# Two attention blocks on one core: two tiles of exponentials in eight computed as a cubic on VectorE and GpSimd, and weights loaded in pieces

## The chip, the cores and the metric

One core of one Trainium2 chip. The time is the device time of one execution in microseconds (us). Engines are named as in the profile: PE (TensorE matmuls), PEld (its weight loads), ACT (ScalarE), DVE (VectorE), POOL (GpSimd), SP (the queue that issues most DMAs).

## What is computed

Two independent blocks over 2048 positions, 1024 features and 32 heads of 32 channels; their outputs are put side by side.

```python
# A: plain attention
q, k, v = split(x @ wqkv)                       # 32 heads
p = softmax(q @ k.T * 32 ** -0.5)               # 2048 x 2048 for each head
out_a = (p @ v) @ wo

# B: four segments of 512 positions, causal inside a segment, with a memory M, z carried over segments
phi = lambda t: where(t > 0, t + 1, exp(t))
a_dot = softmax(q_s @ k_s.T * scale + mask) @ v_s
a_mem = (phi(q_s) @ M) / (phi(q_s) @ z + 1e-6)
o = g * a_mem + (1 - g) * a_dot                 # g = sigmoid(beta)
M = M + phi(k_s).T @ v_s;  z = z + sum(phi(k_s))
out_b = o @ wo
```

The inputs are normal numbers times 0.05 in bf16; the weights of B have another factor of 1/32. Scores are therefore small: for A half the scale times (largest |q|^2 + largest |k|^2) of a group of four heads is between 0.077 and 0.090, worked out from the reference's inputs.

## The kernel before

**Tiles and sets.** Heads are taken four at a time: a group g of A (8 groups) or an index j of B (8 in each of 4 segments). A *unit* of A is a group and a chunk c of 256 queries (64 units); it runs over eight key blocks t of 256 keys. One key block of one unit is a *set*: four tiles, one for each head, each of 128 x 512 scores (two pieces of 128 keys by 256 queries). `plan_set` plans a set: one PE step of eight score matmuls (L821) into four PSUM banks, then two ACTIVATEs with exp (`plan_exp`, L853), each over two banks (1024 columns for A; for B, 1024 or 768), which write bf16 to a ring of 12 buffers P, then the P·V matmuls (L898) and the row sums with a matrix of ones (L904, `plan_pv`). When a unit's last set is done, `norm` transposes the row sums on DVE (L922), takes the reciprocal (L931), spreads it (L933) and multiplies. Units of B lie between those of A. Some of B's tiles are masked on POOL (L864).

**PSUM.** Banks 0 to 5 are three slots of two banks for scores, used in turn: a set takes two slots, so the next set takes the third slot and the first slot of this set. Bank 6 is the only one for *jobs* (projections, output products, guards, memory); a job holds it from its first matmul until DVE has copied it out (L1051 for most; the matmuls have the line of the helper `mm4`, L519). Bank 7 collects P·V and the row sums of a unit.

**Order.** Nothing is ordered by the hardware at run time. The Python program gives each operation a duration, a key and its dependencies, and `schedule` plays the engines forward in a model: PE prefers a score step when it is due (ROW_LEAD ahead of ACT's end), else the best ranked P·V step or job. What comes out is a fixed queue for each engine with semaphore waits. `level` spreads the jobs between their earliest and latest times, `plan_jobs` gives these times; a DMA with `gate=True` waits for the exponential nearest to its key, and all such DMAs go through SP in order.

**Guard.** Exponentials need no maximum subtracted while scores are small. `guard_end` bounds the scores of a group by half the scale times (largest |q|^2 + largest |k|^2). Where the bound exceeds FREE = 40, a flag is raised, ACT branches to a second copy of its program with a bias in each exponential (`alt` in `plan_exp`, `run_split`), and stays there. `square` (L1069, POOL) and the first matmuls of `guard_cols` (L1078) feed it.

**Loads.** The four x_B segments are turned by a DMA transpose (L1035), Wv_B is loaded in halves of 1 MB (`load_WBv`, L1026), W_B in pieces of 256 KB (`load_WB`, L1020). Wo_B (2 MB) is loaded once and stays; Wo_A (2 MB) goes in three DMAs into tiles that are free by then (`load_WoA`). Results leave by `job_out` (L1404) and, for A's attention, through a scratch in HBM (L985).

Of the kernel before, what the change touches and what calls it, by code (L numbers as in the profile page):

```python
# [25 lines left out]
P_RING = 12  # L26
EXP_FIXED = 0.051
FREE = 40.0
# [9 lines left out]
B_STEP3 = 1.133  # L38
# [100 lines left out]
ROW_LEAD = 0.735  # L139
AHEAD = 25  # L140
HEAT = 0.605
STICK = 0.5
# [4 lines left out]
JOB_SLOPE = 0.8  # L147
MARGIN = 0.535
RXJ = 4
RX0 = 80  # L150
LEAD_A, LEAD_B, DUE_AT, DUE_SLOPE = 14.053, 28.135, 19.08, 0.447
HOLD = {}
XR = 11.698
XC = 2.432
# [4 lines left out]
class Prog:  # L159
# [42 lines left out]
    def schedule(self):  # L202
# [19 lines left out]
        for o in self.ops:  # L222
            if pend[o] == 0:
# [4 lines left out]
                            rows=sum(o.urgent is not None for o in self.ops), holder=None)  # L228
# [76 lines left out]
        while left:  # L305
            best = None
            for e, c in cand.items():
                if c:
                    t = max(free[e], min(x.ready for x in c))
                    if best is None or t < best[0]:  # L310
                        best = (t, e)
            t, e = best
            c = cand[e]
            av = [x for x in c if x.ready <= t + 1e-9]
            if e == "PE":
                av = [x for x in av if not opens(x) or opening(x) <= t + 1e-9]
                o = pick(t, av, c)
                if o is None:
                    t2 = [max(free[f], min(x.ready for x in cc)) for f, cc in cand.items() if cc and f != "PE"]
                    t2 += [x.ready for x in c if x.ready > t + 1e-9]  # L320
                    t2 += [v for v in (opening(x) for x in c if opens(x)) if t + 1e-9 < v < 1e9]
                    if t2:
                        free[e] = max(t + 0.02, min(t2))
                        continue
                    o = min(av, key=lambda x: x.key)
            else:
                o = min((x for x in c if x.ready <= t + HOLD.get(e, 0.0)), key=lambda x: x.key - (XR if x.grp is not None else 0.0))
                t = max(t, o.ready)
            d = o.dur
            if e == "PE":  # L330
                ck = clock(t)
                d /= ck
                if o.mode != st["mode"]:
                    t += SWITCH
                st["mode"] = o.mode
                st["rows"] -= o.urgent is not None
                w = o.heat
                st["recent"].append((t, t + d, w * ck))
                k = int(t // WIN)
                st["acts"][k] = st["acts"].get(k, 0.0) + d * w * ck  # L340
                if opens(o):
                    g = st["holder"] = o.grp
                    for h in (0, 1):
                        mine = [x for x in g.pe if h in x.halves]
                        if not mine:
                            continue
                        for x in last[h]:
                            if x not in mine[0].deps:
                                mine[0].deps.add(x)
                                if not x.sched:  # L350
                                    pend[mine[0]] += 1
                                    x.users.append(mine[0])
                        last[h] = [x for x in g.rd if h in x.halves]
                if o.grp is not None:
                    o.grp.left -= 1
            if e == "ACT":
                st["act_end"] = t + d
                if o.prog:
                    st["opn"] += 1
                    st["prog"] = max(st["prog"], o.key)  # L360
            o.start, o.end = t, t + d
            free[e] = o.end
            o.sched = True
            queue[e].append(o)
            c.remove(o)
            left -= 1
            for u in o.users:
                pend[u] -= 1
                if pend[u] == 0:
                    u.ready = ready_of(u) + u.margin  # L370
                    cand[u.eng].append(u)
# [4 lines left out]
    def emit(self, nc, es, block_engines, final_sems):  # L376
        sems = {e: es.enter_context(nc.semaphore("s_" + e)) for e in ("PE", "ACT", "DVE", "POOL")}
        for e in ("ACT", "DVE", "POOL"):
            for n, o in enumerate(self.queue[e]):
                o.pos = n  # L380
                o.deps |= {x for x in o.order if x.eng == e and n - x.pos <= 4}
# [105 lines left out]
class _Kernel:  # L487
# [41 lines left out]

    def build(self):  # L530
# [37 lines left out]
    def alloc(self):  # L568
# [27 lines left out]
        self.WoB = sb("Wo_B", [P, 8, D])  # L596
# [3 lines left out]
        self.r_P = [Res() for _ in range(P_RING)]  # L600
# [178 lines left out]
    def plan_set(self, take, T):  # L779
# [7 lines left out]
        for k, t in enumerate(take):  # L787
            i = bufs[k // 2]
            t["P"], t["n"] = (self.Pt[i], k % 2, self.r_P[i]), n
            self.sets.setdefault(t["set"], []).append(t)  # L790
# [35 lines left out]
        self.item(T, f)  # L826
        for k in range(2):
            self.plan_exp(take[2 * k:2 * k + 2], slots[k], bufs[k], T)
            T += 2 * w / 1200.0 + EXP_FIXED
        self.st.setdefault(take[0]["unit"], T - 2 * (2 * w / 1200.0 + EXP_FIXED))  # L830
        self.en[take[0]["unit"]] = T
        self.plan_pv(take[3], T)
        return T

    def plan_exp(self, take, slot, buf, T):
        w = take[0]["w"]
        cols = 2 * w
        banks = SLOT_BANKS[slot]
        Pt, rP = self.Pt[buf], self.r_P[buf]

        def f(key):
# [3 lines left out]
            if w == 512:  # L845
                src = self.ps[:, c0:c0 + cols]
                dst = Pt.rearrange("p b n -> p (b n)")[:, 0:cols]
            else:
# [4 lines left out]
            a = self.act(guarded if early else lambda e: e.activation(dst, src, ACT.Exp, scale=SCALE), cols, key,  # L853
                         res + [self.r_bias[bc]], [rP], fixed=EXP_FIXED)
            if not early:
                a.alt, a.flag = guarded, self.flag_of[bc]
            a.prog = True
            self.exps.append(a)
            self.exp_keys.append(key)
            nd = sum(p[4] for p in take[0]["pieces"])  # L860
            if nd:
# [3 lines left out]
                                                    channel_multiplier=-1), 2 * nd * P, key + 0.1, [rP], [rP])  # L865
# [157 lines left out]
    def load_WBv(self, s, hh, key):  # L1023
        mark([self.r_WBv], "W", s, hh)
        src = self.B_wv.rearrange("(i p) n -> p i n", p=P)[:, :, 512 * hh:512 * hh + 512]
        self.dma(lambda e: e.dma_start(self.WBv[:, :, :], src), self.sm_WBv, key, [], [self.r_WBv], lat=6.0, gate=True)  # L1026

    def load_xB(self, s, key):
        xb = self.B_x[0]
        mark([self.r_xTB], "x", s)  # L1030
        self.turn(self.xTB[:, :, :], xb[L * s:L * s + L, :], self.sm_xTB, key, [], [self.r_xTB], 5.0, 2.4, True)
# [82 lines left out]
    def guard_end(self, key, cols, nper, bias_cols, bank=None):  # L1114
# [17 lines left out]
        for k, bc in enumerate(bias_cols):  # L1132
# [7 lines left out]
                [self.r_braw], [rb])  # L1140
            nf = self.nflag
# [247 lines left out]
    def job_out(self, kind, row, half, key, lhs, rl, wo, rwo, bank=None, ev="DVE"):  # L1389
# [5 lines left out]
        assert ev == "DVE"  # L1395

        def mm(h, c, r):
            for j in range(8):
                self.pe(lambda e, j=j: self.mm4(e, src[:, c], lhs(j), wo(j)[:, 512 * half:512 * half + 512][:, c],
# [6 lines left out]

    def job_outB(self, s, tt, hf, key):
        rs = [self.r_OTB[j][tt // 2] for j in range(8)]
        holds(rs, "O", s)
        self.job_out("B", 4 * s + tt, hf, key, lambda j: self.OTB[:, j, P * tt:P * tt + P], lambda j: rs[j:j + 1],  # L1410
                     lambda j: self.WoB[:, j, :], lambda j: [self.r_WoB])
# [10 lines left out]
    def load_WoA(self, key):  # L1422
        src = self.A_wo.rearrange("(j p) n -> p j n", p=P)
        for lo, n, dst, rs in ((0, 4, self.VA[0].rearrange("p a b -> p (a b)"), [r for x in self.r_VA[0] for r in x]),
                               (4, 2, self.WA[0].rearrange("p a b c -> p (a b c)"), self.r_WA[0]),
                               (6, 2, self.WA[1].rearrange("p a b c -> p (a b c)"), self.r_WA[1])):
            mark(rs, "Wo")
            self.dma(lambda e, lo=lo, n=n, dst=dst: e.dma_start(dst.rearrange("p (j n) -> p j n", n=D), src[:, lo:lo + n, :]),
                     self.sm_WoA[(lo + 1) // 3], key, [], rs, lat=5.0, gate=True)
# [74 lines left out]
    def plan_jobs(self):  # L1504
# [18 lines left out]
        for c in range(4):  # L1523
            add(p2 + 9.0, st["A", 1, 0] - 1.0, VJ, lambda key, c=c: self.job_V0(1, c, key, None, self.a0_ge))
        self.item(200.0, lambda key: self.dma(lambda e: e.dma_start(
            self.WoB[:, :, :], self.B_wo.rearrange("(j p) n -> p j n", p=P)), self.sm_WoB, key, [], [self.r_WoB], lat=12.0, gate=True))
# [16 lines left out]
        for s in range(NSEG):  # L1543
# [7 lines left out]
            self.item(rx + 0.1, lambda key, s=s: self.load_WBv(s, 0, key))  # L1551
# [12 lines left out]
            for hh in range(2):  # L1564
                r = max(en["B", s - 1, 4 * hh + 3] + 12.0, rx + 12.0) if s else rx + 12.0
                d = SB[0] - 3.0 if hh == 0 else SB[RXJ]
                if hh:
                    self.item(max(r, SB[0] - 2.9) if s else SB[0] - 2.9, lambda key, s=s: self.load_WBv(s, 1, key))
                    r = max(r, SB[0] - 2.9 + 8.0)
                for tt in range(4):  # L1570
                    add(r, d, VJ, lambda key, s=s, tt=tt, hh=hh: self.job_VB(s, tt, hh, key))
            if s:
                for k in range(8):
                    add(end + 3.0, SB[0] - 4.0, OUT, lambda key, s=s, k=k: self.job_outB(s - 1, k // 2, k % 2, key))
# [8 lines left out]
        for k in range(8):  # L1583
            add(en["B", 3, 7] + 3.0, st["A", 7, 6], OUT, lambda key, k=k: self.job_outB(3, k // 2, k % 2, key))

        t7 = st["A", 7, 0]
        self.item(t7 - 6.0, self.load_WoA)
# [20 lines left out]
        for (r, d, c, f), (t, v) in zip(jobs, self.loads):  # L1608
            self.item(t, lambda key, d=d, f=f: self.with_due(d, f, key))

# [48 lines left out]
```

## Time and profile before

| | |
|---|---|
| median of 3 runs | 1160.54 us (1156.72 to 1161.52) |
| the profiled execution | 1161.7 us, span 1160.0 us |
| granted clock of TensorE, mean | 0.995 |
| ACT, exponentials of 1024 columns (L853) | 1080, mean duration 1157 ns |
| ACT, exponentials of 768 columns (L853) | 128, mean duration 966 ns |
| DVE, copies of a job's 512 columns (L1051) | 244, median 692 ns |
| POOL, squares of 512 columns (L1069) | 124, median 1040 ns |
| HBM read, written | 39.00 MB, 11.73 MB |

Busy time is the union of an engine's instructions, so that two that overlap count once. An ACTIVATE overlaps the next, so its duration is longer than what it costs. The ends of matmuls are modelled. "A <- B" in a list of waits means that A stood still until B was done, with the total in us, the number of times and the longest. "issue" is time in which an engine waited for nothing that the profile shows.

### The profile page before, as it was taken

What the parts mean: (1) busy time and instruction counts of PE and PEld (TensorE: products, weight loads), DVE (VectorE), ACT (ScalarE), POOL (GpSimd) and SP (SyncE); (2) the same over time, 40 slices, a digit from 0 to 9 for tenths busy, and PEclk for the clock granted to TensorE, in tenths of its full rate; (3) what the DMA queues carried; (4) which work ended last, traced back from release to release, by engine and by line L of the source; (5) the groups of instructions that cost most, each with busy time, mean ns of one, the idle gap of its engine ahead of it and who ended that gap; (6) DMA issues with size and microseconds to landing.
All of it is one profiled execution on the core that took longest, in us unless ns stands there. A gap on an engine that the chain in (4) does not pass through costs nothing.

```text
span 1160.0 us, 67207 instructions
## 1 busy us (share of the span) xinstructions
PE 1066.1 (92%) x31592; PEld 725.4 (63%) x31592; DVE 602.0 (52%) x1478; ACT 1119.1 (96%) x1256; POOL 222.0 (19%) x279
## 2 busy tenths in 40 slices
PE   7998999999999988989899999899999879999997
PEld 4665666666667656656566666566676546656575
DVE  3353454554563358656733675765526565653233
ACT  3999999999999999999999999999999989999997
POOL 1101133221230222312201330331102230100000
PEclk9999999999999999999999999999999999999999
DMA  9004341135101330032130321320131630000001
GB/s 197 8 12 107 60 117 45 15 92 124 42 15 48 78 96 17 6 90 51 34 81 25 81 54 24 73 59 16 31 77 47 179 89 9 31 31 31 31 27 49
DMA packets 163255, 66.59 MB, mean 57 GB/s; under 512 B 133792, under 2 KB 160160, under 8 KB 162976
## 3 DMA queue, kind: packets, MB, share of 16 engines
q1 hardware_dynamic: 160608, 61.50, 22.0%
q8 instruction: 247, 4.05, 1.5%
q10 hardware_dynamic: 2368, 0.79, 0.3%
q14 instruction: 32, 0.26, 0.1%
HBM read 39.00 MB, written 11.73 MB: 44 GB/s over the span
## 4 chain that ended last, share of the span: by engine, by line
ACT 70%; PE 20%; issue 4%; DVE 3%; DMA 1%; SPq 1%; POOL 0%; ACTq 0%; DVEq 0%
ACT P L853 68%; PE ps L519 11%; PE ps L821 4%; PE ps L898 3%; PE ps L904 2%; ACT PKQ_B L1323 2%; SPq L1035 1%; DMA W_B<-in_B_wk_dram 1%; DMA xT_A<-in_A_x_dram 1%; ACT P L851 0%; DVE KQ_B L1051 0%; DVE T L922 0%; DVE KQ_A L1051 0%; DVE PKQ_B L1328 0%; DVE OTst L981 0%
## 5 line engine op out<-in xcount | busy, mean ns | idle before, releaser
L853 ACT ACTIVATE P<-ps 128x1024 bf16<-128x1024 f32 (+1 forms) x1208 | 1092.2, 1137 | 17.8 <-PE ps L821 14.7
L904 PE MATMUL ps<-P,onesb 128*32 128x256 bf16 (+1 forms) x4864 | 293.0, 270 | 3.8 <-issue 3.8
L898 PE MATMUL ps<-P,V_A 128*32 128x256 bf16 x4096 | 251.0, 274 | 11.2 <-ACT P L853 9.0
L821 PE MATMUL ps<-KQ_A 32*128 32x256 bf16 x4096 | 205.2, 273 | 32.0 <-ACT P L853 24.1
L821 PEld LDWEIGHTS ps<-KQ_A 32*128 32x128 bf16 x4096 | 61.2, 92 | 146.2 <-ACT P L853 123.6
L519 PE MATMUL ps<-xT_B,W_B 128*32 128x256 bf16 x4096 | 141.2, 278 | 8.6 <-DMA W_B<-in_B_wk_dram 2.5
L864 POOL TENSOR_SCALAR_AFFINE_SELECT P<-P 128x512 bf16<-128x512 bf16 x128 | 86.6, 686 | 313.9 <-ACT P L853 309.9
L519 PE MATMUL ps<-xT_A,W_A 128*32 128x256 bf16 (+1 forms) x3968 | 136.7, 277 | 7.6 <-DVE KQ_A L1051 2.5
L898 PEld LDWEIGHTS ps<-P,V_A 128*32 128x32 bf16 x4096 | 110.5, 96 | 50.3 <-ACT P L853 21.5
L904 PEld LDWEIGHTS ps<-P,onesb 128*32 128x32 bf16 x4864 | 132.2, 97 | 9.6 <-issue 4.9
L519 PEld LDWEIGHTS ps<-xT_B,W_B 128*32 128x32 bf16 x4096 | 100.9, 97 | 38.9 <-issue 27.2
L1069 POOL TENSOR_TENSOR sqB<-KQ_B 128x512 bf16<-128x512 bf16 x64 | 68.0, 1063 | 284.9 <-DVE KQ_B L1051 254.3
L519 PEld LDWEIGHTS ps<-xT_A,W_A 128*32 128x32 bf16 x3968 | 97.1, 96 | 36.1 <-issue 19.6
L1069 POOL TENSOR_TENSOR sqA<-KQ_A 128x512 bf16<-128x512 bf16 x60 | 63.4, 1057 | 224.5 <-DVE KQ_A L1051 202.2
L1051 DVE CAST KQ_B<-ps 128x512 bf16<-128x512 f32 x64 | 44.2, 691 | 115.0 <-PE ps L519 113.2
L1051 DVE CAST outsb<-ps 128x512 bf16<-128x512 f32 x56 | 38.6, 690 | 112.0 <-PE ps L519 111.9
L922 DVE STREAM_TRANSPOSE T<-ps 128x256 f32<-128x256 f32 (+1 forms) x148 | 72.1, 487 | 43.0 <-PE ps L904 22.3
L1051 DVE CAST KQ_A<-ps 128x512 bf16<-128x512 f32 x60 | 41.5, 691 | 86.9 <-PE ps L519 86.5
L933 DVE STREAM_TRANSPOSE T<-rc 128x256 f32<-128x256 f32 (+1 forms) x152 | 73.0, 482 | 3.1
L519 PE MATMUL ps<-Wo_B,OT_B 128*32 128x256 bf16 x2048 | 73.2, 274 | 0.7 <-DVE outsb L1051 0.5
L519 PE MATMUL ps<-Wv_B,xT_B 128*32 128x256 bf16 x2048 | 69.4, 274 | 1.3 <-DVE KQ_B L1051 1.1
L519 PEld LDWEIGHTS ps<-Wo_B,OT_B 128*32 128x32 bf16 x2048 | 48.8, 96 | 18.2 <-issue 11.0
(96 smaller groups left out, 947.6 us busy)
## 6 DMA issues: line engine op xcount, KB each, us to landing
Wv_B<-in_B_wv_dram SPq DMA_DIRECT2D x8, 1024.0 KB, 6.3
W_B<-in_B_wk_dram SPq DMA_DIRECT2D x32, 256.0 KB, 3.4
W_B<-in_B_wq_dram SPq DMA_DIRECT2D x32, 256.0 KB, 4.2
out_dram<-outsb SPq DMA_DIRECT2D x56, 128.0 KB, 1.8
W_A<-in_A_wqkv_dram SPq DMA_DIRECT2D x14, 256.0 KB, 3.9
ot_a_scratch<-OTst SPq DMA_DIRECT2D x51, 64.0 KB, 2.2
xT_A<-ot_a_scratch SPq DMA_DIRECT2D x6, 512.0 KB, 8.6
Wo_B<-in_B_wo_dram SPq DMA_DIRECT2D x1, 2048.0 KB, 9.3
```

Of the source, the lines that this page charges most:

```text
L519: ins = e.matmul(out[r], w[:, r], x, start=start, stop=stop, tile_position=(0, 32 * t), skip_group_check=True)
L821: ins = e.matmul(out, kap, qap, start=st, stop=True, tile_position=(32 * h, 0), skip_group_check=True)
L853: a = self.act(guarded if early else lambda e: e.activation(dst, src, ACT.Exp, scale=SCALE), cols, key, res + [self.r_bias[bc]], [rP], fix ...
L864: self.pool(lambda e: e.affine_select(v, v, pattern=pat, compare_op=ALU.is_ge, fill=0.0, base=0, channel_multiplier=-1), 2 * nd * P, key + ...
L898: ins = e.matmul(self.ps[32 * h:32 * h + 32, 512 * obk + q0:512 * obk + q0 + nq], vt[:, c0 + 32 * h:c0 + 32 * h + 32], Pt[:, b, off:off + nq],
L904: ins = e.matmul(self.ps[32 * h:32 * h + 32, lcol + q0:lcol + q0 + nq], self.onesb[:, 0:32], Pt[:, b, off:off + nq], start=False, stop=las ...
L922: self.dve(lambda e: e.transpose(T1[:, 0:n], src), n, key, rsrc, [r1], fixed=0.17)
L933: self.dve(lambda e: e.transpose(T2[:, 0:n].rearrange("p (b r) -> p b r", r=32), bc), n, key, [rr], [r2], fixed=0.17)
L1035: return self.dma(lambda e: e.dma_start(dst, src, transpose=True), sem, key, reads, writes, issue=issue, lat=lat, gate=gate)
L1051: self.dve(lambda e: e.tensor_copy(dst, src), 512, key, [self.at(b)], rdst)
L1069: self.pool(lambda e: e.tensor_tensor(sq[:, :], src, src, ALU.mult), 512, key, [rsrc], [rs], rate=0.5)
L1323: x = self.act(lambda e: e.activation(PKQ[:, a:b, :], src, ACT.Exp), n, key, rs, rp[a:b], fixed=0.19)
```

## The change

- In sets of A with t = 1 or 4 (units that are not computed in parts), the tile of the first head is taken from ACT. DVE reads its bank and writes Y, linear in the scores, in f32; POOL makes Z = (Y + a) * Y in two instructions; DVE writes P = (Z + b) * Y in bf16: a cubic near exp. ACT's first exponential of such a set has 512 columns instead of 1024.
- FREE goes from 40 to 1/8. In ACT's second program a later ACTIVATE (the second one of the third set on) first redoes the tile as an exponential of Y. The operation's dependencies are the same in both programs.
- P·V of such a set is planned 4.7 us later; each half of a P buffer has its own record of readers and writers; exponentials keep their planned order.
- An engine other than PE may pass over the operation with the lowest key when an urgent one (a cube's first step) becomes ready before it would end (SOON).
- Wo_B has half its size and is loaded in halves for each segment; output products of B go half by half. Wv_B, Wo_B and Wo_A are loaded in pieces of 256 KB, one every 1.78 or 2.23 us of planned time (`pieces`). x_B's first segment is loaded at 31.9 instead of 80 of planned time.
- Planner constants are changed.

```diff
-FREE = 40.0
+FREE = 0.125
+KAPPA, ROOT, CUBE_A, CUBE_B = 0.5501767600212002, -1.5993248390626598, -0.9857377158509045, 1.2295944671136563
+CUBIC = (1, 4)
+CUBE_POS = 0
+CARRY = 7
+CUBE_PV = 4.7
+BCK = 7.199
+POOLED = True
+SOON = 0.192
-B_STEP3 = 1.133
+B_STEP3 = 1.144
-ROW_LEAD = 0.735
+ROW_LEAD = 0.862
-STICK = 0.5
+STICK = 0.681
-JOB_SLOPE = 0.8
-MARGIN = 0.535
+JOB_SLOPE = 0.773
+MARGIN = 2.914
-RX0 = 80
-LEAD_A, LEAD_B, DUE_AT, DUE_SLOPE = 14.053, 28.135, 19.08, 0.447
+RX0 = 31.858
+LEAD_A, LEAD_B, DUE_AT, DUE_SLOPE = 14.503, 30, 22.842, 0.552
-XR = 11.698
-XC = 2.432
+XR = 12
+XC = 2.558
+STEP = 1.779
+OUT3 = 55.232
+WOA_STEP = 2.232
...
@@ schedule
                 o = min((x for x in c if x.ready <= t + HOLD.get(e, 0.0)), key=lambda x: x.key - (XR if x.grp is not None else 0.0))
+                soon = min((x for x in c if x.urgent), key=lambda x: x.ready, default=None)
+                if soon is not None and soon.ready < max(t, o.ready) + o.dur - SOON:
+                    o = soon
...
+    def pieces(self, key, step, fns, sem, writes, tag, lat):
...
+        for n, fn in enumerate(fns):
+            self.item(key + n * step, lambda key, fn=fn, n=n: piece(key, fn, n))
...
-        self.WoB = sb("Wo_B", [P, 8, D])
+        self.WoB = sb("Wo_B", [P, 8, 512])
...
@@ plan_set
+        cube = kind == "A" and take[0]["part"] is None and take[0]["set"][3] in CUBIC
+        fix = self.fixes.pop(n - 1, None)
+        if cube:
+            self.fixes[n - 1 + CARRY - CARRY % 2] = self.plan_cube(take[CUBE_POS], banks[CUBE_POS], T)
         for k in range(2):
-            self.plan_exp(take[2 * k:2 * k + 2], slots[k], bufs[k], T)
-            T += 2 * w / 1200.0 + EXP_FIXED
+            lo, hi = (int(cube and 2 * k == CUBE_POS), 2 - int(cube and 2 * k + 1 == CUBE_POS))
+            self.plan_exp(take[2 * k:2 * k + 2], slots[k], bufs[k], T, lo, hi, fix if k == CARRY % 2 else None)
+            T += (hi - lo) * w / 1200.0 + EXP_FIXED
...
-        self.plan_pv(take[3], T)
+        self.plan_pv(take[3], T + (CUBE_PV if cube else 0.0))
...
+    def plan_cube(self, t, bank, T):
...
+            o = self.dve(lambda e: e.tensor_scalar(Y[:, :], src, KAPPA * SCALE, -KAPPA * ROOT, ALU.mult, ALU.add), 512, key - 9.0,
+                         [self.bank[bank]], [rY])
+            o.urgent = True
+            if POOLED:
+                self.pool(lambda e: e.tensor_scalar(Z[:, :], Y[:, :], CUBE_A, None, ALU.add), 512, key - BCK, [rY], [rZ], rate=0.5)
+                self.pool(lambda e: e.tensor_tensor(Z[:, :], Z[:, :], Y[:, :], ALU.mult), 512, key - BCK, [rY, rZ], [rZ], rate=0.5)
...
+            self.dve(lambda e: e.scalar_tensor_tensor(out=dst, in0=Z[:, :], scalar=CUBE_B, in1=Y[:, :], op0=ALU.add,
+                                                      op1=ALU.mult), 512, key - BCK, [rY, rZ], [rP])
...
@@ plan_exp
+            rd, wr = res + [self.r_bias[bc]], list(rP)
+            alt = guarded
+            if fix is not None:
+                redo, bcf, rY, rPf = fix
+                rd += [rY, self.r_biasr[bcf]]
+                wr.append(rPf)
...
-        self.dma(lambda e: e.dma_start(self.WBv[:, :, :], src), self.sm_WBv, key, [], [self.r_WBv], lat=6.0, gate=True)
+        self.pieces(key, STEP, [lambda e, i=i: e.dma_start(self.WBv[:, i:i + 2, :], src[:, i:i + 2, :]) for i in range(0, 8, 2)],
+                    self.sm_WBv, [self.r_WBv], ("W", s, hh), 4.0)
...
@@ plan_jobs
-        self.item(200.0, lambda key: self.dma(lambda e: e.dma_start(
-            self.WoB[:, :, :], self.B_wo.rearrange("(j p) n -> p j n", p=P)), self.sm_WoB, key, [], [self.r_WoB], lat=12.0, gate=True))
...
+    def outB(self, add, cost, s, r, d):
+        m = r + 0.45 * (d - r)
+        self.load_WoB(s, 0, r - 5.0 - 3 * STEP)
+        self.load_WoB(s, 1, m + 0.5)
+        for hf, lo, hi in ((0, r, m), (1, m + 5.5 + 3 * STEP, d)):
+            for tt in range(4):
+                add(lo, hi, cost, lambda key, hf=hf, tt=tt: self.job_outB(s, tt, hf, key))
```

## The prediction

> **What bounds the kernel now.** I read the page's busy times first, then the groups, the waits, the ACT timeline, and last the chain of waits where ACT stood still.
>
> ```profile
> PE 1066.1 (92%) x31592; PEld 725.4 (63%) x31592; DVE 602.0 (52%) x1478; ACT 1119.1 (96%) x1256; POOL 222.0 (19%) x279
> ...
> ACT 70%; PE 20%; issue 4%; DVE 3%; DMA 1%; SPq 1%; POOL 0%; ACTq 0%; DVEq 0%
> ```
>
> ACT is busy for 96% of the span and carries 70% of the chain that ended last. PE's 92% looks nearly as high, but the waits say who is ahead:
>
> ```profile
> PEld ps L821 <- ACT P L853: 149.0, 493, 1.3
> ...
> PE ps L821 <- ACT P L853: 28.6, 74, 1.0
> ...
> ACT P L853 <- PE ps L821: 14.7, 17, 2.9
> ```
>
> The score matmuls (L821) waited 149.0 + 28.6 = 178 us for ACT to give banks back, ACT 14.7 us for scores. ACT sets the pace; PE has some slack, though not in every stage (PE was busy 56.84 of 58 us from 348 to 406).
>
> ```profile
> 315.35 1.28 ACT L1323 ACTIVATE PKQ_B<-KQ_B 128x1024 bf16<-128x1024 bf16 x1
> 316.30 1.74 ACT L853 ACTIVATE P<-ps 128x768 bf16<-128x768 f32 x2
> 317.68 1.30 ACT L1323 ACTIVATE PKQ_B<-KQ_B 128x1024 bf16<-128x1024 bf16 x1
> ```
>
> What an exponential costs ACT is the distance of two starts, not its duration, since neighbours overlap: two of 768 columns took 317.68 - 316.30 = 1.38 us, 0.690 each. Of the 1035 neighbouring pairs of 1024 columns in the timeline the median distance is 0.904. So 256 columns cost 0.213, one column 0.832 ns, and an instruction 0.05 besides.
>
> Where ACT did stand still, the chain names PE, and PE names nothing ("issue"):
>
> ```profile
> 927.86 0.11 PE ps L898 x4
> 928.07 3.13 issue
> 931.20 0.30 PE ps L904 x2
> ```
>
> ```profile
> 926.00:932.00 6.00, 2.87 (x84) 1.72 (x72) 1.18 (x4) 3.14 (x5) 2.23 (x3) 1.00 0.89 332
> ```
>
> In that stretch (columns: PE, PEld, DVE, ACT, POOL busy, granted clock, DMA share, GB/s) PE did 2.87 of 6 us with the clock at 1.00, while DMA ran at 0.89 and 332 GB/s: Wo_A's 2 MB, asked for at once. The like stands at 240.3 (1.42 us of issue, 236 GB/s from 234 to 240), 267.1 (1.04, 273 GB/s from 262 to 268) and 917.7 (0.98, 333 GB/s from 912 to 920). At 107.8 the chain runs 7.0 us through W_B's load, queued behind x_B's transpose and the 1 MB Wv_B. ACT's gaps at these places (113.7, 120.1, 239.5, 266.8, 917.2, 923.7, 928.1 and 934.6) sum to 13 us.
>
> **The change, part by part.** The sum is made against the profiled execution: 1161.7 us, of which 1160.0 is span. That is 1.2 over the median.
>
> *Columns taken from ACT.* Of the 64 units of A, the first four go in parts and are left alone; 60 units x 2 key blocks = 120 tiles. In each, one ACTIVATE of 1024 columns becomes one of 512: 0.904 - (0.05 + 512 x 0.832 ns) = 0.426 us. All of it lies on the path: 120 x 0.426 = **-51.1**. Instruction count stays. The one 512-column ACTIVATE from PSUM that the trace has a distance for (L1497, 0.494) agrees nearly: with it -49.2.
>
> *The guard.* FREE = 1/8 must not be passed, else the other instruction stream runs. From the reference's inputs, half the scale times (largest |q|^2 + largest |k|^2) of a head group is at most 0.090 in A and below 0.001 in B, so the plain stream runs. The flag is read by ACT before too: 0. The few added one-column instructions on DVE (0.15 to 0.2 us by L1138 and L1135, two to a group) go beside: 0.
>
> *The cubes on DVE and GpSimd.* DVE's first step reads 512 f32 of PSUM: 0.69 by L1051. Its closing step has two f32 SBUF inputs of 512: L998 takes 0.424 for 256, and 256 more at the rate of L1051 give 0.69. GpSimd's product is 1.04 by L1069; its one-input step lies between 0.64 (L864) and 1.04; I take 0.8. DVE: 602 + 120 x 1.38 = 768 us, near 69% of a shorter span; GpSimd: 222 + 120 x 1.84 = 443, 40%. Both stay under ACT: 0 for the busy time, which is hidden beside ACT and PE. If that cover goes (casts of job bank 6 queued behind a cube's two DVE steps), each cast that is late holds PE's next job by up to 0.69.
>
> *The wait for the bank.* This is the new cost on the path. The scores of set n+1 are one PE step over four banks, two of which are the first pair of set n. Before, that pair came back with one ACTIVATE, 0.90 after its start. Now ACT's half is back after 0.48 and DVE's after its step of 0.69. By the trace, scores end a median of 0.12 us ahead of their ACTIVATE. So with DVE free the bank is back about 0.7 after ACT's start, handing over included. The two ACTIVATEs end at 1.38; the score step takes 0.33 (L821 x8 in the chain) and about 0.1 to hand over (an estimate: the shortest lead of the scores is 0.05), so it must start by about 0.95. That leaves a quarter of a microsecond. A full DVE step of 0.69 in front turns into 0.45 of ACT standing still. Bounds: 0 and 120 x 0.45 = +54; below 0 is excluded, since the bank cannot come back before ACT needs it read. The change makes DVE hold back for an urgent step (SOON = 0.19), so I stay near the low end: 0.1 each, **+12**. Queued behind the waiting score step on PE are all P·V and job matmuls.
>
> *The late tile and the carried wait.* The chain of a cube is 0.69 + 0.8 + 1.04 + 0.69 = 3.2 us and four hand-overs, some 4 us. P·V of that set is put off by 4.7. In the program the second ACTIVATE of the third set after it also waits for the closing step (it would redo the tile in the guarded stream). It starts 1.38 + 2 x 1.81 + 0.90 = 5.9 us after the cube's set: 2 us to spare. Bounds 0 and, if each chain ran 2.5 us late, 120 x 0.5 = +60; I take 0. All later exponentials stand behind that wait.
>
> *Loads.* Wv_B in four, Wo_A in eight pieces of 256 KB, x_B's first load at 32 instead of 80 in plan time, so that its transpose no longer stands ahead of W_B at the last moment. The 13 us above are what is at stake; the stall at 934.6 also had a clock of 0.72, and x_B's transposes stay whole, so I take **-10** (bounds 0 and -13). What is late next there is the job bank, and jobs are spread by level(). Wo_B by halves loads 8 MB in 32 pieces instead of 2 MB once. With Wv_B (8 to 32) and Wo_A (3 to 8) that is 60 issues more on SP, at 0.3 to 0.6 us. SP spends its time waiting (283 us for OTst alone), and behind it stand only stores and later loads. A 256 KB W_B lands in 3.4 to 4.2, so the last of four pieces 1.78 apart is there after about 9.5, against 6.3 for 1 MB now; the jobs' earliest times are moved by more. 0; bounds 0 and +8 (eight loads late by 1 us).
>
> *PE closer to ACT.* The same PE work in 4% less time: 1066.1 us busy is 92% now and 95.6% of a span of 1115. ACT's remaining small gaps grow: **+4**, bounds 0 and +25 (the 178 us of slack used up in the full stages). The retuned planner constants have no row; they are inside these bounds.
>
> Sum: 1161.7 - 51.1 - 10 + 12 + 4 = 1116.6; less 1.2 for the median: **1115**.
>
> **The rivals.** *PE becomes the bound.* For: 98% busy in one stage. Against: 178 us of waits on ACT, and a stage at 98% shows that it can be run so. If PE's mean share rises only to 93.5%, the time is 1066.1 / 0.935 = 1140.
>
> *DVE hands the banks back late* (slower). The place is the first step of each cube. For: one DVE step in front already costs 0.45 of the 0.43 gained, and the trace shows DVE steps held far longer than their own work:
>
> ```profile
> 324.43 1.53 DVE L1328 SCALAR_TENSOR_TENSOR PKQ_B<-KQ_B,PKQ_B 128x512 bf16<-128x512 bf16 x1
> ...
> 325.89 0.68 DVE L1328 SCALAR_TENSOR_TENSOR PKQ_B<-KQ_B,PKQ_B 128x512 bf16<-128x512 bf16 x1
> ```
>
> ```profile
> 324.20 1.21 POOL L1069 TENSOR_TENSOR sqA<-KQ_A 128x512 bf16<-128x512 bf16 x1 [2.24 <-DVE KQ_A L1051]
> ```
>
> The same instruction took 1.53 us beside GpSimd's 1.21 and 0.68 after it. With GpSimd at 40% instead of 19%, two-input steps meet it twice as often, 120 new ones among them. From 0.43 of stall per cube the gain is gone (the loads' 10 us put the turn at 0.51). At 0.65 it is 1161.7 - 51.1 - 10 + 78 - 1.2 = 1177. Against: the first step itself has one input, from PSUM, and L1051 reads 0.69 in every case. The Trainium skill's page "SBUF — State Buffer", section "Who interferes with whom", has this as a rule: a DVE instruction with two SBUF inputs and a GpSimd instruction that reads SBUF exclude each other for the whole instruction. The trace agrees, with 1.53 against 0.68; by that rule alone this rival's 1177 would be the time.
>
> *Loads were more of it than I credit, and the banks cost nothing*: 1161.7 - 51.1 - 13 - 1.2 = 1096.
>
> *The guard trips after all, and the change doesn't do what it says*: every cube is redone on ACT, 0.48 more each than now forecast, 120 x 0.48 + 1115 = 1173.
>
> **How the numbers follow.** Forecast (1100 to 1130) 0.58; PE bound (1130 to 1154) 0.14; better than 1100 0.07; a mixture within 0.5% of 1160.5 (no measurement of this kernel can tell less from no change) 0.05; banks late 0.14; guard 0.02. Faster by over 0.5%: 0.58 + 0.14 + 0.07 = 0.79; slower 0.16. The range takes in the forecast with its bounds, the PE case and half of the better one: 1094 to 1152.
>
> **What would show it.** Right: 120 ACTIVATEs of 512 columns, the next one starting 0.48 later; ACT busy near 1068 and still about 95% of the span; DVE near 770, GpSimd near 440; no "issue" of 3 us where Wo_A is loaded; W_B's load off the chain; the bank wait as L821 waiting for DVE's first step, some tens of us on PE and about 12 on ACT. Wrong: ACT idle time ended by DVE or by L821 of more than 50 us; PE waits on ACT near zero with "issue" or job waits in their place; ACTIVATEs waiting for the cubes' closing step; instructions with a bias operand after the first parts (guard tripped).

## The result, and the profile after

The changed kernel takes 1165.97 us (median; 1162.48 to 1168.84) against 1159.78: a ratio of 1.0053, 95% interval 1.0035 to 1.0071. It is slower by half a per cent where 1115 was forecast. The profiled execution, the shortest of seven, took 1162.48 us, span 1160.6. Ratios leave out slow executions; without the one of 1428.78 us among its four, the median 1143.55 further down would be 1143.16. Line numbers have moved: exponentials L853 are L938, scores L821 are L863, row sums L904 are L992, job copies L1051 are L1139, POOL's squares L1069 are L1157, and two of DVE's steps in B's normalisation, L996 and L998, are L1084 and L1086. New are L895 (a cube's first step), L899 and L900 (POOL's two steps) and L904 (the closing step).

The page, busy times and the chain by engine:

```profile
PE 1054.4 (91%) x31592; PEld 729.6 (63%) x31592; DVE 813.1 (70%) x1726; ACT 1079.0 (93%) x1256; POOL 560.9 (48%) x519
...
PE 42%; DVE 28%; ACT 19%; POOL 5%; issue 4%; SPq 1%; DMA 1%; DVEq 0%; ACTq 0%; POOLq 0%
```

ACT gave up what it was meant to: there are 120 ACTIVATEs of 512 columns, the next one starts 0.477 us later in the median, and busy time fell from 1119 to 1079 us (1068 was forecast; an ACTIVATE with no neighbour behind it counts with its whole duration). But the span did not follow. ACT has 19% of the chain instead of 70%, DVE 28% instead of 3%. ACT now stands still. Its waits:

```profile
ACT P L938 <- PE ps L992: 23.7, 24, 3.3
ACT P L938 <- PE ps L863: 20.9, 47, 1.3
...
ACT P L938 <- DVE P L904: 4.9, 10, 0.6
```

Before, exponentials waited 14.7 us for scores and nothing for row sums (a wait for those is a buffer of P that P·V has not yet given back). A sharper count: take the distance of each two neighbouring starts on ACT, less the shortest distance of that form (0.903, 0.690, 0.477, ...). What is left over sums to 57.9 us before and to 108.8 after (waits of the first 30 us among them). The 51 us taken from ACT came back as 51 us of gaps.

POOL's two steps, as minimum, median and maximum in ns:

```profile
L899 POOL TENSOR_SCALAR Z<-Y x120: 1484/1488/1856, 88.4 to 1143.7; 128x512 f32<-128x512 f32 x120
```

```profile
L900 POOL TENSOR_TENSOR Z<-Z,Y x120: 1263/1274/1722, 90.8 to 1145.3; 128x512 f32<-128x512 f32 x120
```

I had priced them at 0.8 and 1.04 us. DVE's steps with two inputs in SBUF became longer, those that the change does not touch among them. The groups before, then after (busy us, mean ns of one):

```profile
L996 DVE SCALAR_TENSOR_TENSOR T<-T,gc 128x256 f32<-128x256 f32 x48 | 23.0, 479 | 1.0
...
L998 DVE TENSOR_TENSOR OT_B<-T,OT_B 128x256 bf16<-128x256 f32 x48 | 20.0, 417 | 0.8
```

```profile
L904 DVE SCALAR_TENSOR_TENSOR P<-Z,Y 128x512 bf16<-128x512 f32 x120 | 101.4, 845 | 53.1 <-POOL Z L900 46.9 <-issue 4.5 <-ACT P L938 0.7
...
L1084 DVE SCALAR_TENSOR_TENSOR T<-T,gc 128x256 f32<-128x256 f32 x48 | 37.5, 781 | 0.8
...
L1086 DVE TENSOR_TENSOR OT_B<-T,OT_B 128x256 bf16<-128x256 f32 x48 | 30.9, 643 | 0.6
```

Ten microseconds of the timeline show how this reaches ACT: first DVE, then POOL, then PE, then ACT.

```profile
539.99 0.42 DVE L1086 TENSOR_TENSOR OT_B<-T,OT_B 128x256 bf16<-128x256 f32 x1
...
543.50 0.98 DVE L1084 SCALAR_TENSOR_TENSOR T<-T,gc 128x256 f32<-128x256 f32 x1
544.51 1.39 DVE L1086 TENSOR_TENSOR OT_B<-T,OT_B 128x256 bf16<-128x256 f32 x1
545.83 0.68 DVE L1139 CAST KQ_B<-ps 128x512 bf16<-128x512 f32 x1
```

```profile
541.71 1.49 POOL L899 TENSOR_SCALAR Z<-Y 128x512 f32<-128x512 f32 x1 [2.03 <-DVE Y L895]
543.16 1.04 POOL L1157 TENSOR_TENSOR sqB<-KQ_B 128x512 bf16<-128x512 bf16 x1
544.16 1.47 POOL L900 TENSOR_TENSOR Z<-Z,Y 128x512 f32<-128x512 f32 x1
```

```profile
546.56 0.95 PE L534 MATMUL ps<-xT_B,W_B 128*32 128x256 bf16 x28 [0.73 <-DVE KQ_B L1139]
```

```profile
549.64 1.02 ACT L938 ACTIVATE P<-ps 128x1024 bf16<-128x1024 f32 x1 [2.45 <-PE ps L992]
```

L1086 takes 0.42 us with POOL idle and 1.39 with L900 beside it, ending 0.27 after L900 does. The copy that empties the job bank (L1139) stands behind it on DVE, PE waits 0.73 us for that copy, and the job's matmuls stand on PE in front of the P·V and row sums that give ACT a buffer back: ACT stands still for 2.45 us, until 549.64. Of these, 0.73 is PE's wait for the copy; the rest is PE's own work in its fixed order. The two stages of the prediction's load stalls, by the same columns as there:

```profile
926.00:932.00 6.00, 4.54 (x140) 3.07 (x136) 5.72 (x9) 4.34 (x5) 2.81 (x3) 1.00 0.95 299
104.00:122.00 18.00, 17.72 (x393) 12.55 (x389) 11.62 (x33) 17.14 (x22) 8.28 (x6) 1.00 0.03 7
```

PE did 4.54 us instead of 2.87 in the first, and ACT's idle time from 912 to 938 fell from 6.1 to 2.9 us. From 104 to 122 PE did 17.72 at a clock of 1.00 (before: 13.03 at 0.81), but the loads of that stage are now issued from 55 to 73 us, and there ACT stands still for 3.33 us at 62.2 and 1.45 at 73.6, where it did not before. No wait of PE for W_B is left. So the stalls named in the prediction are smaller or gone, and the sum gained little by it.

### The profile page after: what moved, and what is told of

Same layout as the page of the kernel before. It is cut to its first block, busy times and chain, and to the rows that moved or that the text cites. A ratio compares the mean times of both kernels' runs of the same rounds, so it can differ in the third digit from the quotient of the medians.

```text
span 1160.6 us, 67980 instructions
## 1 busy us (share of the span) xinstructions
PE 1054.4 (91%) x31592; PEld 729.6 (63%) x31592; DVE 813.1 (70%) x1726; ACT 1079.0 (93%) x1256; POOL 560.9 (48%) x519
## 4 chain that ended last, share of the span: by engine, by line
PE 42%; DVE 28%; ACT 19%; POOL 5%; issue 4%; SPq 1%; DMA 1%; DVEq 0%; ACTq 0%; POOLq 0%
PE ps L534 23%; ACT P L938 19%; PE ps L863 8%; PE ps L986 5%; PE ps L992 5%; DVE P L904 4%; DVE Y L895 3%; POOL Z L899 2%; DVE T L1010 2%; POOL Z L900 2%; DVE T L1084 2%; DVE OT_B L1086 2%; DVE T L1021 2%; DVE PKQ_B L1419 2%; DVE KQ_A L1139 1%
## 5 line engine op out<-in xcount | busy, mean ns | idle before, releaser
L938 ACT ACTIVATE P<-ps 128x1024 bf16<-128x1024 f32 (+2 forms) x1208 | 1048.3, 1015 | 55.9 <-PE ps L992 23.7
L899 POOL TENSOR_SCALAR Z<-Y 128x512 f32<-128x512 f32 x120 | 180.2, 1502 | 279.6 <-DVE Y L895 272.5
L992 PE MATMUL ps<-P,onesb 128*32 128x256 bf16 (+1 forms) x4864 | 291.2, 270 | 1.4 <-issue 1.4
L863 PE MATMUL ps<-KQ_A 32*128 32x256 bf16 x4096 | 204.9, 273 | 36.4 <-ACT P L938 24.0
L900 POOL TENSOR_TENSOR Z<-Z,Y 128x512 f32<-128x512 f32 x120 | 158.2, 1318 | 7.9
L863 PEld LDWEIGHTS ps<-KQ_A 32*128 32x128 bf16 x4096 | 62.3, 92 | 148.8 <-ACT P L938 99.8
L952 POOL TENSOR_SCALAR_AFFINE_SELECT P<-P 128x512 bf16<-128x512 bf16 x128 | 83.4, 659 | 135.2 <-ACT P L938 131.3
L534 PE MATMUL ps<-xT_B,W_B 128*32 128x256 bf16 x4096 | 137.6, 274 | 9.3 <-DVE KQ_B L1139 4.0
L904 DVE SCALAR_TENSOR_TENSOR P<-Z,Y 128x512 bf16<-128x512 f32 x120 | 101.4, 845 | 53.1 <-POOL Z L900 46.9
L992 PEld LDWEIGHTS ps<-P,onesb 128*32 128x32 bf16 x4864 | 131.3, 97 | 8.6 <-issue 2.2
L1157 POOL TENSOR_TENSOR sqA<-KQ_A 128x512 bf16<-128x512 bf16 x60 | 65.9, 1098 | 103.1 <-DVE KQ_A L1139 86.5
L895 DVE TENSOR_SCALAR Y<-ps 128x512 f32<-128x512 f32 x120 | 81.6, 680 | 30.2 <-PE ps L863 28.8
L1157 POOL TENSOR_TENSOR sqB<-KQ_B 128x512 bf16<-128x512 bf16 x64 | 71.9, 1124 | 55.8 <-DVE KQ_B L1139 53.6
L1139 DVE CAST KQ_A<-ps 128x512 bf16<-128x512 f32 x60 | 41.2, 686 | 49.7 <-PE ps L534 49.4
```

The lines of the kernel that those rows point to most:

```text
L534: ins = e.matmul(out[r], w[:, r], x, start=start, stop=stop, tile_position=(0, 32 * t), skip_group_check=True)
L863: ins = e.matmul(out, kap, qap, start=st, stop=True, tile_position=(32 * h, 0), skip_group_check=True)
L895: o = self.dve(lambda e: e.tensor_scalar(Y[:, :], src, KAPPA * SCALE, -KAPPA * ROOT, ALU.mult, ALU.add), 512, key - 9.0, [self.bank[bank]] ...
L899: self.pool(lambda e: e.tensor_scalar(Z[:, :], Y[:, :], CUBE_A, None, ALU.add), 512, key - BCK, [rY], [rZ], rate=0.5)
L900: self.pool(lambda e: e.tensor_tensor(Z[:, :], Z[:, :], Y[:, :], ALU.mult), 512, key - BCK, [rY, rZ], [rZ], rate=0.5)
L904: self.dve(lambda e: e.scalar_tensor_tensor(out=dst, in0=Z[:, :], scalar=CUBE_B, in1=Y[:, :], op0=ALU.add, op1=ALU.mult), 512, key - BCK, ...
```

## The experiments

Each kernel's order is planned anew by the same program, so that two variants differ in more than the edited line. The size of this is seen below: moving P·V alone changed the time by 6 us. A difference of a few microseconds is therefore read only where a trace shows its place. Ratios are to the kernel before, with 95% intervals; it was run again beside each group of variants (medians 1157.3 to 1159.5 us), so the ratios are the better scale between groups.

**The cubes taken out, the rest kept.**

```diff
-CUBIC = (1, 4)
+CUBIC = ()
```

> The changed kernel without any cube: every exponential goes back to ACT; the loads in pieces, Wo_B by halves, the guard and the planner's constants stay. Three theories stand for the lost 51 us. (1) Late tiles: GpSimd's two f32 steps measured 1.49 and 1.27 us (I had 0.8 and 1.04), a cube takes 5.2 us in the median instead of 4, and P.V and the carried wait stand behind it. (2) Full VectorE: 813 us of work at 70%, with steps lengthened beside GpSimd, makes job copies, bank hand-backs and normalisations late, whether the cube itself is late or not. (3) The rest of the change (loads, constants) costs what the cubes bring. By (1) and (2) this kernel is at 1145 to 1160 (before, less some of the 13 us of load stalls); by (3) it is at 1190 or more, 1166 and the 51 us that ACT gets back minus nothing.

Measured: 1162.33, ratio 1.0032 (1.0013 to 1.0051). The third theory falls: the rest does not cost 51 us. But it does not bring 10 either. ACT's left-over distances sum to 57.3 us, as before (57.9): of the load stalls one of 1.55 us is left (at 925), and a new stall has come. The chain at 57 us:

```profile
57.91 0.70 DVE cols L1173
58.66 0.28 PE ps L1371 x2
58.97 0.40 PE ps L863 x8
59.36 2.67 PE ps L1371 x24
```

L1371 are A's first V jobs. P·V needs their result, P buffers stay full, and the exponential after the one that starts at 60.3 comes 5.2 us late.

**x_B's first load back at its old place**, without cubes.

```diff
-RX0 = 31.858
+RX0 = 80
```

> e1_no_cubes with x_B's first load at 80 of planned time, as before the change. e1 was no faster than before (1162.3 against 1159.3) although its load stalls are gone; it has a new stall of 5.2 us at 60.3 us and two smaller ones, where A's V jobs stand late among B's first jobs. If that early load made them: 1154 to 1158. If the pieces themselves cost it: 1160 to 1163.

Measured: 1158.28, ratio 0.9984 (0.9966 to 1.0001). The stalls at 60 us are gone, so the early x_B made them (B's first jobs in front of A's V jobs), at some 4 us. Against before, pieces and constants are then worth 1 to 2 us, not 10, and the interval reaches no gain at all. ACT still loses 2.5 us at 913 and 1.7 at 510.

**POOL's steps moved to DVE.**

```diff
-POOLED = True
+POOLED = False
```

> The cube's two GpSimd steps become one more VectorE step of about 0.69 us; the chain is three VectorE steps, about 2.2 us without queueing, and VectorE's work grows to about 602 + 120 x 2.06 = 849 us, less what it lost beside GpSimd. (1) late tiles: faster than after, 1120 to 1145. (2) full VectorE: no faster than after, 1160 to 1185. (3) the rest: about 1160 to 1170, no change.

Measured: 1157.16, ratio 0.9986 (0.9966 to 1.0006). 9 us better than the change although DVE does 120 steps more, its busy time rising only from 813 to 823. That speaks against a full DVE as such; but the forecast of the late-tile theory (1120 to 1145) was not met either.

**POOL's steps left out.** The closing step reads Y in place of Z.

```diff
-            if POOLED:
-                self.pool(lambda e: e.tensor_scalar(Z[:, :], Y[:, :], CUBE_A, None, ALU.add), ...
-                self.pool(lambda e: e.tensor_tensor(Z[:, :], Z[:, :], Y[:, :], ALU.mult), ...
...
-            self.dve(lambda e: e.scalar_tensor_tensor(out=dst, in0=Z[:, :], scalar=CUBE_B, in1=Y[:, :], ...
+            self.dve(lambda e: e.scalar_tensor_tensor(out=dst, in0=Y[:, :], scalar=CUBE_B, in1=Y[:, :], ...
```

> GpSimd's two steps are left out and the closing step reads Y alone, so P in these tiles is a square instead of a cubic; VectorE's two steps and all else stay. VectorE then has about 765 us of work instead of 813 (nothing is lengthened beside the cubes' GpSimd steps). (1) late tiles: 1115 to 1140, since the chain is 1.4 us. (2) full VectorE: most of the loss stays, 1150 to 1165. (3) no change from 1166.

Measured: 1143.55, ratio 0.9862 (0.9815 to 0.9908). 22 us better than the change: POOL's two steps cost that, by lateness or otherwise.

**POOL's steps done, but nobody waits for them**: the closing step as in the last kernel, the first edit undone.

> GpSimd does its two steps on Y as in the changed kernel (240 instructions, some 340 us), but the closing step reads Y alone, so nobody waits for them (the tile is a square instead of a cubic). It separates the two ways in which GpSimd's 22 us between 1166 (changed) and 1143.5 (e3_no_z) can come about. If the lateness of the tile costs them: near 1143. If GpSimd's work itself costs them, by lengthening VectorE's two-input steps (closing step 0.69 alone, 1.51 beside GpSimd, and L1084, L1086 from 0.48 and 0.42 to 0.78 and 0.64): near 1160 to 1166. In between: both.

Measured: 1163.69, ratio 1.0041 (1.0014 to 1.0068). All but 2 us of the loss is back, with a tile that is in time (2.0 us from L895's start to L904's end in the median, 5.1 in the changed kernel). POOL's work is enough for the loss; lateness is not needed.

**The same POOL time without reading.**

```diff
-                self.pool(lambda e: e.tensor_scalar(Z[:, :], Y[:, :], CUBE_A, None, ALU.add), ...
-                self.pool(lambda e: e.tensor_tensor(Z[:, :], Z[:, :], Y[:, :], ALU.mult), ...
+                for _ in range(5):
+                    self.pool(lambda e: e.memset(Z[:, :], 0.0), 512, key - BCK, [rY, rZ], [rZ], rate=1.6)
```

> e5_z_unused with GpSimd's two steps replaced by five memsets of Z (some 0.5 us each, estimated from L719's 0.206 for 128 columns): GpSimd is as busy and its other work queues as long, but it reads nothing from SBUF. VectorE's two-input steps have a partner to exclude only while GpSimd reads. If e5's 20 us over e3 (1163.7 against 1143.5) come from that exclusion: 1140 to 1150, with L1084 and L1086 back near 0.48 and 0.42. If they come from GpSimd's own queue (masks and squares late): 1158 to 1166.

Measured: 1145.38, ratio 0.9883 (0.9822 to 0.9943). POOL is busy for 532 us (573 in the kernel before it), and it costs 2 us instead of 20. The groups of three kernels: POOL's steps left out, POOL reading, the memsets (busy us, mean ns; L898, L1078 and L1080 are L904, L1084 and L1086 in the first of the three):

```profile
L898 DVE SCALAR_TENSOR_TENSOR P<-Y 128x512 bf16<-128x512 f32 x120 | 88.4, 737 | 1.9
...
L1078 DVE SCALAR_TENSOR_TENSOR T<-T,gc 128x256 f32<-128x256 f32 x48 | 23.4, 488 | 0.6
...
L1080 DVE TENSOR_TENSOR OT_B<-T,OT_B 128x256 bf16<-128x256 f32 x48 | 21.7, 451 | 0.2
```

```profile
L904 DVE SCALAR_TENSOR_TENSOR P<-Y 128x512 bf16<-128x512 f32 x120 | 96.4, 804 | 1.6
...
L1084 DVE SCALAR_TENSOR_TENSOR T<-T,gc 128x256 f32<-128x256 f32 x48 | 43.0, 896 | 0.6
...
L1086 DVE TENSOR_TENSOR OT_B<-T,OT_B 128x256 bf16<-128x256 f32 x48 | 31.7, 660 | 0.2
```

```profile
L900 POOL MEMSET Z<- 128x512 f32 x600 | 315.8, 526 | 291.1 <-DVE Y L895 258.9 <-DVE rc L1019 3.2 <-DVE flags L1234 2.2
...
L904 DVE SCALAR_TENSOR_TENSOR P<-Y 128x512 bf16<-128x512 f32 x120 | 87.7, 730 | 1.7
...
L1084 DVE SCALAR_TENSOR_TENSOR T<-T,gc 128x256 f32<-128x256 f32 x48 | 23.7, 493 | 0.6
...
L1086 DVE TENSOR_TENSOR OT_B<-T,OT_B 128x256 bf16<-128x256 f32 x48 | 22.1, 459 | 0.2
```

L1084 falls from 896 to 493 ns and L1086 from 660 to 459; before the change they were 479 and 417. With the memsets the three steps take what they take when POOL's steps are left out. The page "SBUF — State Buffer" of the Trainium skill, section "Who interferes with whom", says that a DVE instruction with two SBUF inputs contends with a POOL instruction that reads SBUF and not with one that only writes it. The last two kernels agree with it: 1163.69 reading, 1145.38 writing.

**The late tile by itself**: memsets, and the closing step waits for them.

```diff
-            ... e.scalar_tensor_tensor(out=dst, in0=Y[:, :], scalar=CUBE_B, in1=Y[:, :], ... [rY], [rP])
+            ... e.scalar_tensor_tensor(out=dst, in0=Z[:, :], scalar=CUBE_B, in1=Y[:, :], ... [rY, rZ], [rP])
```

> e9_memset (GpSimd writes only, 5 memsets) with the closing step waiting for them, so that the tile is as late as in the changed kernel (some 5 us) while the cube's GpSimd steps read nothing. e9 without the wait was 1145.4. Lateness costs nothing: 1143 to 1150. Lateness costs what I read from the carried wait and the P.V behind it: 1152 to 1166.

Measured: 1155.95, ratio 0.9967 (0.9946 to 0.9988). The tile takes 4.8 us in the median. So lateness has a price too, about 10 us when POOL's steps exclude nobody; with exclusion there it added 1 to 2 (1163.69 to 1165.97), which a newly planned order alone can make. The two losses overlap.

**One step only**: DVE writes a line, 1 + the scaled score, straight to P; closing step, POOL's steps and the redo in ACT's second program are left out.

```diff
-            o = self.dve(lambda e: e.tensor_scalar(Y[:, :], src, KAPPA * SCALE, -KAPPA * ROOT, ALU.mult, ALU.add), 512, key - 9.0,
-                         [self.bank[bank]], [rY])
+            o = self.dve(lambda e: e.tensor_scalar(dst, src, SCALE, 1.0, ALU.mult, ALU.add), 512, key - 9.0,
+                         [self.bank[bank]], [rP])
...
+        return None
```

> A cube is one VectorE step only: it writes 1 + the scaled score straight to P (a line instead of a cubic); closing step, GpSimd's steps and the carried redo are left out. What is left of the price is the bank that waits for that step. VectorE has about 685 us of work. By (1) and by (2) alike this is the ceiling of the idea: 1105 to 1130 (prediction's sum without late tiles: 1115). If it stays above 1145, the wait for the bank or PE's own load eats the gain, or (3).

Measured: 1134.55, ratio 0.9779 (0.9741 to 0.9818). Faster than before by 2.2%, and 4.6 us above the range that I gave as the ceiling.

**No step at all**: nobody computes the tile.

```diff
-            src = self.ps[:, 512 * bank:512 * bank + 512]
-            o = self.dve(lambda e: e.tensor_scalar(dst, src, SCALE, 1.0, ALU.mult, ALU.add), ...
-            o.urgent = True
+            pass
```

> Nobody computes the tile: ACT's 120 instructions stay narrow, VectorE's step is left out too (P keeps old values there). Nothing waits for a bank but for ACT. e4_one_step (1134.5) less the price of the bank's wait: 1115 to 1123 if I had that term right (12 us and more); 1130 to 1136 if the wait costs nothing and PE with its one job bank holds the rest.

Measured: 1127.03, ratio 0.9740 (0.9681 to 0.9798). It lies between the two forecasts. The bank's wait with the step itself costs some 5 to 8 us (by the ratios and by the medians), which is near what a newly planned order alone can make; without it, 16 of the 51 us are still missing.

**Less work for PE**, with the one step.

```diff
-            for j in range(8):
+            for j in ((0, 7) if kind == "B" else range(8)):
                 self.pe(lambda e, j=j: self.mm4(e, src[:, c], lhs(j), wo(j)...
```

> e4_one_step with a quarter of the matmuls of B's output product: 32 jobs x 12 steps of four matmuls at 0.109 us, 42 us less for PE, spread over four segments; the rest is as in e4. If what e4 misses (1134.5 against 1111) is PE and its job bank: 1115 to 1125. If it is the bank's wait for VectorE: 1130 to 1136.

Measured: 1120.29, ratio 0.9673 (0.9614 to 0.9732). B's output product sums two of eight blocks of heads here. PE's busy time falls by 36 us (42 was the estimate) and the time by 12 to 14: PE, with the single bank that its jobs share, has become a bound once ACT has less to do. Which of the two it is stays open, since the shorter jobs also give the bank back sooner.

**The fourth head's tile instead of the first's**, with the one step and with the whole cubic.

```diff
-CUBE_POS = 0
+CUBE_POS = 3
```

> e4_one_step with the fourth head's tile instead of the first's. Its bank lies in the set's second slot, which the next set's scores do not need; the set after that needs it, one ACTIVATE pair later. If what e4 still loses (1134.5 against 1111, which is e1's 1162.3 less 51.1) is the wait for the bank: 1115 to 1125. If it is PE's own load or the late P.V: 1130 to 1137. P.V is planned 4.7 us late in both.

> The changed kernel, whole cubic, with the fourth head's tile instead of the first's: no next set waits for VectorE's first step. The late tile and GpSimd's work stay. By the prediction's rival (banks late) most of the loss is there: 1130 to 1145. By late tiles or by VectorE beside GpSimd: 1155 to 1166, at most the 20 us of PE's waits for L895 less.

Measured: 1145.06, ratio 0.9870 (0.9829 to 0.9912), and 1190.04, ratio 1.0275 (1.0232 to 1.0318): 10 and 24 us worse. I had the wrong wait. The next set's scores need the first slot back, and are made while ACT does the second. With the fourth head that second ACTIVATE is the narrow one: the score step of 0.33 us and its hand-overs must fit into 0.48 instead of 0.90. ACT's waits for scores, the first head's kernel and then the fourth's, both with the one step:

```profile
ACT P L929 <- PE ps L863: 14.0, 22, 3.2
```

```profile
ACT P L929 <- PE ps L863: 18.7, 50, 3.3
```

22 waits become 50. These lists leave out waits under 0.15 us; the distances of starts say more. Behind a narrow ACTIVATE the next one starts 0.477 us later in the median with the first head's tile and 0.706 with the fourth's (0.724 with the whole cubic): over the 120 of them 31 us more than with the first head (37 with the cubic), of the 51 that they were to save. Behind the wide ones the one-step kernel gets 26 us of this back, the cubic 7.

**P·V not put off**, with the one step.

```diff
-CUBE_PV = 4.7
+CUBE_PV = 0.0
```

> e4_one_step with CUBE_PV = 0: P.V of a cube's set is planned when its exponentials are done and not 4.7 us later, as the one-step tile is early enough. In e4 ACT waited 25.9 us for row sums (P buffers not yet free). If the late P.V costs that: 1115 to 1125. If the bank or PE's load: 1130 to 1137.

Measured: 1140.92, ratio 0.9834 (0.9791 to 0.9877). 6 us slower instead of faster: the late P·V was not what the one-step kernel lost.

**The one step in three key blocks, with the planner's constants chosen again.** The kernel sets the constants anew below the old ones; here as old and new.

```diff
-CUBIC = (1, 4)
+CUBIC = (1, 4, 6)
-CUBE_PV = 4.7
+CUBE_PV = 0.0
-RX0 = 31.858
+RX0 = 45.0
-STICK, PV_ROOM, JOB_AT, LEAD_A, DUE_AT, XR, XC, STEP = 0.681, 6.294, -0.354, 14.503, 22.842, 12, 2.558, 1.779
+STICK, PV_ROOM, JOB_AT, LEAD_A, DUE_AT, XR, XC, STEP = 0.652, 6.329, -0.367, 13.426, 25.878, 12.758, 2.388, 1.622
...
```

> A version meant to beat both: e4_one_step (the tile is one VectorE step, a line under the guard of 1/8) in three key blocks of eight (1, 4, 6) instead of two, P.V not put off (CUBE_PV = 0), x_B's first load at 45 instead of 31.9 of planned time (at 31.9 B's first jobs crowd out A's V jobs and ACT waits 5 us at 60 us), and the planner's other constants chosen again for it: STICK, LEAD_A, DUE_AT, STEP, XR, XC, SOON. ACT gives up 180 x 0.426 = 77 us instead of 51. If PE and its one job bank are what is left: 1120 to 1130, most of the third tile lost again. If ACT's load still decides: 1105 to 1115.

Measured: 1126.87, ratio 0.9704 (0.9681 to 0.9727), the fastest kernel here that computes every tile. It is the one-step kernel with three key blocks; under the guard of 1/8 the line is off by at most 0.9% (the next term of the series is 1/128). It lacks the redo, as do the other one-step kernels: for scores beyond the guard, where the changed kernel computes the tile again as an exponential, the line stays. What the redo's wait costs is in no run by itself. Against the one-step kernel with two blocks ACT gave up 25.6 us more and the time fell by 8, new constants included, as the PE-bound case had it. The later x_B load did not help: ACT still stands still for 4.7 us at 61.5.

## Why the prediction was wrong, by its own steps

- *Columns taken from ACT, -51.1*: right as a size; the distance behind a narrow ACTIVATE is 0.477 us. "All of it lies on the path" was not: with the tile left to nobody a third is missing (below, PE).
- *The guard, 0*: right; the plain stream ran (L938 has no bias operand; L926, with one, ran in the first parts alone).
- *"Both stay under ACT: 0 for the busy time"*: this step failed. POOL's steps took 1.49 and 1.27 us instead of 0.8 and 1.04 (I took bf16 rows for f32 work), POOL was busy 561 us instead of 443, DVE 813 instead of 768, and the 45 us more on DVE are steps that became longer (L904 18 us against 0.69 each, L1084 14.5, L1086 11). The cost was not 0 but 20 us (1143.55 to 1163.69 with a tile in time; 10 when the tile is late anyway, 1155.95 to 1165.97). I had the mechanism, with L1328's 1.53 us, but as a rival placed at the cubes' first step. L895 never took more than 0.694. The instructions that pay have two inputs in SBUF: B's normalisation (L1084 479 to 781 ns, L1086 417 to 643), and the closing step (845 in the mean, 692 in the median). None of them stands in the printed chain of before. Now job copies and normalisations stand behind them on DVE, and PE's jobs and the P buffers behind those; the timeline from 540 to 550 us shows it at one place, and DVE's 28% of the chain says that it is not the only one.
- *The wait for the bank, +12*: the right place, as PE's waits for L895 in the changed kernel show (13.2 us before weight loads, 6.4 before matmuls), but about half the size: 5 to 8 us (1127.03 without the step, 1134.55 with it).
- *The late tile, 0*: wrong, some 10 us alone, 1 to 2 on top of the exclusion. The chain was not 4 us but 5.1 in the median, from L895's start to L904's end.
- *Loads, -10*: the stalls named there are smaller or gone, as forecast, but some 4 us are lost to the early x_B load, which I had counted as a help only, and most of the rest to other places. With x_B late the loads and constants are worth 1 to 2 us.
- *PE closer to ACT, +4*: mis-sized. 1162.33 less 51.1 is 1111; with the tile left to nobody it was 1127: 16 us, inside the bounds of 0 to 25. That the 16 are PE and its job bank is argued from the kernel with less work for PE.

In ratios to before, times 1159.3 to put all runs on one scale, and each kernel planned anew: without cubes 1163.0; less 51.1 is 1111.9; PE and its job bank +17.3 (no step, 1129.2); DVE's one step +4.5 (1133.7); the closing step and the carried wait +9.6 (1143.3); POOL reading +20.8 (1164.1); the late tile +1.3 (1165.4). The rows sum to 53.5 and take back what ACT gave. The split depends on the order: with the late tile first it is memsets +2.4, the late tile +9.7, POOL reading +10.0.

Of the rivals, PE becoming the bound took a third. The banks handed back late gave the sign, not the place: the exclusion it named is real, but it cost 10 to 21 us on two-input steps and not 78 on the cubes' first step, which has one input. That the kernel came out slower, as this rival said, is therefore luck. The closing step and the carried wait were not told apart from each other.

## What to carry to other kernels

Before work moves from a bound engine to idle ones, count what the receiving engines share: two engines at 70% and 48% that exclude each other in some instructions are fuller than their busy times say, and the bill comes on old instructions that nobody edited. Take a duration from a row with the same type, not only the same size. And when the bound engine gives up 5%, ask how much slack the next one has in the full stages; here PE's 178 us of waits hid that only two thirds of the 51 us could be had with this plan.

## What was not expected of the hardware

- POOL's one-input step on f32 (512 columns, 1.49 us) is slower than its two-input product on f32 (1.27), while its masks on bf16 with one input take 0.64 (L952, median) and its bf16 product 1.04.
- POOL writing without reading costs DVE's two-input steps little (L1084 493 against 479 ns before), but a DVE step with one input, L1416 on 1024 bf16, becomes longer beside memsets too: 415 to 419 ns with POOL idle, 518 to 835 in the seven cases in which it met memsets alone.
